# Decode attention and feed-forward on one core: two units per softmax, score products of 512 columns, V behind the next pair's K

## The chip, the core and the metric

The kernel runs on one of the eight cores of one Trainium2 chip. A core has five engines with instruction queues of their own: PE (TensorE, matrix products), DVE (VectorE), ACT (ScalarE), POOL (GpSimd) and SP (SyncE, which here issues all the transfers). Sixteen DMA engines move data between the chip's memory (HBM) and the core's on-chip memory; products are accumulated in PSUM, which has eight banks of 512 fp32 values per partition, over 128 partitions.

The metric is the device time of one execution in microseconds. Before the change three runs gave 654.61, 655.31 and 655.44 us; the median is 655.31.

## The reference: what is computed

One token of each of four sequences goes through two identical layers of attention and feed-forward (the weights and the cache of both layers are the same arrays):

```python
B, Sq, D = 4, 1, 512
Hq, Hkv, Sk, Dh = 32, 8, 8192, 128          # 4 query heads share one key/value head

def _A_ref(x, k_cache, v_cache, wq, wo):
    q = (x @ wq).reshape(B, Sq, Hq, Dh).transpose(0, 2, 1, 3)
    k = jnp.repeat(k_cache, 4, axis=1)
    v = jnp.repeat(v_cache, 4, axis=1)
    scores = jnp.einsum("bhqd,bhkd->bhqk", q, k) * (Dh ** -0.5)
    p = softmax(scores, axis=-1)
    o = jnp.einsum("bhqk,bhkd->bhqd", p, v)
    return o.transpose(0, 2, 1, 3).reshape(B, Sq, Hq * Dh) @ wo

def _B_ref(x, w_gate, w_up, w_down):        # F = 1792
    return (silu(x @ w_gate) * (x @ w_up)) @ w_down

for _ in range(2):
    x = x + _A_ref(layernorm(x), k_cache, v_cache, wq, wo)
    x = x + _B_ref(layernorm(x), w_gate, w_up, w_down)
```

All arrays are bf16. Both caches together have 4 x 8 x 8192 x 128 x 2 values, 134 MB, and each layer needs all of them.

## The kernel before, in words

**Units.** A unit is one pair of a sequence and a key/value head: 32 units per layer, numbered u = 4 * head + sequence. A unit's K is 2 MB and so is its V: 8192 rows, of which partition p holds 64 consecutive ones. On chip there are eight slots of 2 MB (`kv`, slots 0 to 7), each for one K or one V.

**Loads.** `work(L)` (L270) gives the order of a layer's K and V: K0, K1, V0, K2, V1, K3, V2 and so on; V trails K by a unit. Layer 1 begins with the units 29, 30 and 31, whose K and V stay in slots 0 to 5 from the end of layer 0 (`kept`), so only 58 of its 64 tiles are loaded. `items` is the list of all loads of both layers, with the feed-forward weights (`wg`, `wu`, `wd`) behind the last V of each. `pump()` (L316) walks along it and issues the next load on SP's queue whenever a slot is free; `finished()` (L363) frees a slot when PE has used its tile. The feed-forward weights lie in slots 6 and 7, so the last loads of a layer (`late`, L329) must take slots below 6. The last V of a layer comes in four quarters (`split`), and two tiles at the start of layer 1 come in two halves, each as soon as half of a kept K has been scored (`halves`, `half`, L350). SP executes its issues in order: a load that waits for its slot holds all the loads behind it.

**A unit's work.** `keys` (L473) cuts K into eight blocks. Per block DVE transposes 32x32 tiles in place (`turn`, L396), and PE makes four products (`scores`, L414) with the four heads' queries as the fixed operand, set by POOL into a field of zeros (`zq`, `place_q`), and 256 columns of K as the moving one. Each unit's scores fill one of two PSUM banks as 128 x 256: row 4q + h holds block q and head h. Then the softmax runs in five steps, threaded between the next unit's blocks: `max_p` (DVE, maximum per row), `max_t` (a PE transpose, a DVE maximum per head, an ACT copy), `exps` (a PE product that spreads the maximum, three ACT instructions), `turn_p` (DVE transposes P into one of two halves of `pT`), `total` (a PE sum and a DVE reciprocal). `values` (L496) multiplies P by V in 16 products that lie on four column groups of PE; ACT, DVE and one more product (`own_first`, `own_others`, `add_rows`) add up the four partial sums. The last two units of a layer use `block_last` instead, 64 small products each. After every fourth unit `out_proj` adds the head's share of the output projection to x.

**The order.** The program text decides it. Blocks wait in a list `blocks`, softmax steps in `line`, the steps behind V in `after`; each has a nominal duration, and `advance` (L382) takes steps out when enough nominal time has gone by. Transposes run ahead of the blocks by two nominal microseconds (`LAG`). `flush` forces steps out that must precede others.

**The seam.** `ffn` (L647) needs x after the last unit, so the last V, the output projection, w_gate, w_up and w_down follow each other; layer 1's first two K take slots 6 and 7, so they wait until the feed-forward's products have been made.

Of the kernel before, what the change touches and what calls it, by code (L numbers as in the profile page):

```python
# [103 lines left out]
def bass_interleave_layers__gqa_block_cached__swiglu_ffn__decode_kernel(  # L104
# [18 lines left out]
    P = 128  # L123
# [9 lines left out]
    assert NB * REP == QB and 2 * 2 * QB == Dh  # L133
    SW = TB * QB
# [7 lines left out]
    NV = NB // 2  # L142
    assert TB == 2 * NA and NV * REP <= QB
# [4 lines left out]
    with ExitStack() as es:  # L148
# [8 lines left out]
        kvf = sb("kvf", [P, NSLOT * SL + FR * F], BF16)  # L157
# [3 lines left out]
        wu_sb = [kvf[:, NSLOT * SL + k * F:NSLOT * SL + (k + 1) * F] for k in range(FR)]  # L161
        wu_sb.append(kvf[:, f0 + KT * F:f0 + (KT + 1) * F])
        f1 = f0 + (KT + 1) * F
        assert f1 + FO * D <= NSLOT * SL
# [3 lines left out]
        at_w = {"wg": room(f0, f0 + KT * F) + ["wg"], "wu": room(f0 + KT * F, f1) + ["wu", "wu3"],  # L168
# [8 lines left out]
        one = sb("one", [P, 7], FP32)  # L177
        onesf, eps_sb, lsc_sb, zero_sb, mx, nm, rs = (one[:, i:i + 1] for i in range(7))
        quad = sb("quad", [P, NA], BF16)
        head = sb("head", [P, REP], FP32)  # L180
        xs = sb("xs", [P, B], FP32)
# [6 lines left out]
        own = sb("own", [P, NV], FP32)  # L188
        xc, xx = acc[:, 0:XB], acc[:, XB:2 * XB]
        zq = sb("zq", [P, 4, ZP + P], BF16)  # L190
        m4 = sb("m4", [1, REP], FP32)
        rsm = sb("rsm", [P, REP], FP32)
        pb = sb("pb", [P, SW], BF16)
        mrow = pb[0:1, :].bitcast(FP32)
        pT = sb("pT", [P, 2, SW], BF16)
        qT = pT[:, 1, 0:XQ].rearrange("p (b h) -> p b h", b=B)
        rl = sb("rl", [P, 3, REP], FP32)
# [15 lines left out]
        def bank_bf(k):  # L213
# [14 lines left out]
                 for n, c in (("wq", KT), ("wo", 4), ("wg", 1), ("wu", 2), ("wd", 3))}  # L228
# [11 lines left out]
        for a in range(NA):  # L240
# [8 lines left out]
             reads=["ident"], writes=["head"])  # L249
        T.op("dve", lambda e: e.tensor_reduce(acc[:, 0:QB], identf[:].rearrange("p (y h) -> p y h", h=REP), AX.X, ALU.max),  # L250
             reads=["ident"], writes=["acc"])
        T.op("dve", lambda e: e.tensor_reduce(own[:], acc[:, 0:QB].rearrange("p (a y) -> p y a", a=NA)[:, 0:NV, :],
# [7 lines left out]
        turn_of = {}  # L260
        rl_of = {}
# [8 lines left out]
        def work(L):  # L270
            us, seq = unit_order[L], []
            for i, u in enumerate(us):
                seq.append(("K", L, u))
                if 1 <= i < NU - 2:
                    seq.append(("V", L, us[i - 1]))
            return seq + [("V", L, u) for u in us[NU - 3:]]
# [16 lines left out]
        def load_weight(name, i=0):  # L293
# [8 lines left out]
            elif name == "wg":  # L302
                T.dma("sp", wg_sb, B_w_gate.rearrange("(kt p) f -> p kt f", p=P), sem_w["wg"][0], writes=places + ["wg"])
            elif name == "wu":
                if i == 0:
                    T.dma("sp", kvf[:, NSLOT * SL:].rearrange("p (k f) -> p k f", k=FR),
                          B_w_up[0:FR * P, :].rearrange("(kt p) f -> p kt f", p=P), sem_w["wu"][0], writes=["wu"])
                T.dma("sp", wu_sb[FR], B_w_up[FR * P:, :], sem_w["wu"][1], writes=["wu3"])
            else:

                for j, (a, b) in enumerate(WD):
                    T.dma("sp", wd_sb[:, a:b, :].rearrange("p (m e) n -> p m (e n)", e=2),
                          B_w_down[a * P:b * P, :].rearrange("(m p e) n -> p m (e n)", p=P, e=2), sem_w["wd"][j],
                          writes=[f"wd{j}"])

        def pump():  # L316
            while issued[0] < len(items):
# [11 lines left out]
                late = any(e - 10 < n < e for e in ends)  # L329
# [52 lines left out]
        def advance(us):  # L382
            for steps in (line, after):
                if steps:
                    steps[0][0] -= us
                    while steps and steps[0][0] <= 0:
# [17 lines left out]
        def place_q(u, eng="pool", src=qr, keys_=SCR):  # L404
# [4 lines left out]
            dst = zq[:, :, ZP:].rearrange("p c (a x) -> p c a x", a=NA)[:, :, :, 0:REP]  # L409
# [4 lines left out]
        def scores(L, u, q):  # L414

            s = slot_of["K", L, u]
            bk = SBK[turn_of[u]]
            w = kv[:, s, q * TB * Dh:(q + 1) * TB * Dh].rearrange("p (t c i e) -> p t c i e", t=TB, c=2, e=2)
            z0 = ZP - REP * q
            for c in range(4):  # L420
                T.op("pe", lambda e: e.matmul(bank(bk)[:, 0:SW], lhsT=zq[:, c, z0:z0 + P], rhs=w[:, :, c // 2, :, c % 2],  # L421
                                              start=(q == 0 and c == 0), stop=(q == NB - 1 and c == 3)),
                     reads=[f"s{s}.{q}", "zq"], writes=[f"pb{bk}"], sig=(c == 3))

        def max_p(u):
            bk = SBK[turn_of[u]]
# [3 lines left out]
        def max_t(u):  # L430
# [3 lines left out]
            T.op("dve", lambda e: e.tensor_reduce(m4[:], bank(STEP)[0:1, 0:P].rearrange("p (x h) -> p h x", h=REP),  # L434
                                                  AX.X, ALU.max, negate=True),
                 reads=[f"pb{STEP}"], writes=["m4"])
            T.op("act", lambda e: e.activation(mrow.rearrange("p (x h) -> p x h", h=REP),  # L437
                                               m4[:].unsqueeze(1).to_broadcast([1, QB, REP]), ACTF.Copy),
                 reads=["m4"], writes=["pb"])

        def exps(u):
            bk = SBK[turn_of[u]]
# [3 lines left out]
            by = rstd[:, u % B:u % B + 1]  # L446
            T.op("act", lambda e: e.activation(nm[:], bank(STEP)[:, 0:1], ACTF.Copy, scale=by), reads=[f"pb{STEP}", "rstd"],  # L447
                 writes=["nm"])
            T.op("act", lambda e: e.activation(pb[:], bank(bk)[:, 0:SW], ACTF.Exp, bias=nm[:], scale=by, accum_out=rs[:]),  # L449
                 reads=[f"pb{bk}", "nm", "rstd"], writes=["pb", "rs"])  # L450
            T.op("act", lambda e: e.activation(rsm[:], head[:], ACTF.Copy, scale=rs[:]), reads=["head", "rs"], writes=["rsm"])  # L451

        def turn_p(u):
            T.op("dve", lambda e: e.transpose(pT[:, turn_of[u], :], pb[:]), reads=["pb"], writes=[f"pT{turn_of[u]}"])  # L454

        def total(u):
            T.op("pe", lambda e: e.matmul(bank(TOT)[:, 0:REP], lhsT=ones, rhs=rsm[:], start=True, stop=True),  # L457
                 reads=["rsm", "onesf"], writes=[f"pb{TOT}"])
            T.op("dve", lambda e: e.reciprocal(rl[:, rl_of[u], :], bank(TOT)[:, 0:REP]), reads=[f"pb{TOT}"],  # L459
                 writes=[f"rl{rl_of[u]}"])  # L460
# [12 lines left out]
        def keys(L, u):  # L473
            def block(q):
# [6 lines left out]
                if q == NB // 2 - 1 and ("K", L, u) in halves:  # L481
                    half(("K", L, u), 0)
                if q == NB - 1:
                    finished(("K", L, u))
                    for gap, fn in ((0.0, max_p), (1.0, max_t), (0.9, exps), (1.0, turn_p), (0.3, total)):
                        line.append([gap, u, lambda fn=fn: fn(u)])

            for q in range(NB):
                if (L, u, q) not in turned:
                    turn(L, u, q)  # L490
                blocks.append((0.65, lambda q=q: block(q)))
                drain(LAG)
# [3 lines left out]
        def values(L, u):  # L496
            g, b = unit_gb(u)
            bk = OBK[turn_of[u]]

            def begin():  # L500
                flush(line, u)
                flush(after, turn_of[u])

            def end():
                finished(("V", L, u))
                after.extend(rest)

            def block(i):
# [4 lines left out]
                v = kv[:, s, :].rearrange("p (q t d) -> p t q d", t=TB, d=Dh)  # L513
                for t in range(TB):
                    j = t % NA
                    c0 = t * QB + i * NV * REP
                    T.op("pe", lambda e: e.matmul(bank(bk)[j * QB:j * QB + NV * REP, :],  # L517
                                                  lhsT=pT[:, turn_of[u], c0:c0 + NV * REP], rhs=v[:, t, NV * i:NV * (i + 1), :],
                                                  start=(i == 0 and t == j), stop=(i == 1 and t >= TB - NA)),
# [241 lines left out]
```

## Time and profile before

| | us |
|---|---|
| median of three runs | 655.31 |
| the profiled execution, its own time | 655.51 |
| its span in the trace | 653.7 |
| PE busy, products (4896 instructions) | 500.5 |
| DVE busy (1079) | 446.1 |
| ACT busy (391) | 116.4 |
| K transposes on DVE, 488 of 686 ns | 322.4 |
| score products on PE, 2048 of 256 columns | 346.2 |
| V products, 960 of 512 columns on four column groups | 68.5 |
| P transposes on DVE, 64 of 405 ns | 25.9 |

Busy time of a pipelined PE is the time in which any product is under way; the mean duration of one product (314 ns for a score product) is longer than its share of the busy time. In the profile, "DVE kvf L401" means the DVE instruction of line 401 that writes the tile `kvf`; "<-DMA kvf<-in_A_k_cache_dram" behind a wait means that a load of K ended it. SPq is SP's queue. Granted clock is the share of full speed that the clock throttle allowed PE. HBM was read at 419 GB/s over the span, 273.88 MB in all.

### The profile page before, as it was taken

What the parts mean: (1) busy time and instruction counts of PE and PEld (TensorE: products, weight loads), DVE (VectorE), ACT (ScalarE), POOL (GpSimd) and SP (SyncE); (2) the same over time, 40 slices, a digit from 0 to 9 for tenths busy, and PEclk for the clock granted to TensorE, in tenths of its full rate; (3) what the DMA queues carried; (4) which work ended last, traced back from release to release, by engine and by line L of the source; (5) the groups of instructions that cost most, each with busy time, mean ns of one, the idle gap of its engine ahead of it and who ended that gap; (6) DMA issues with size and microseconds to landing.
All of it is one profiled execution on the core that took longest, in us unless ns stands there. A gap on an engine that the chain in (4) does not pass through costs nothing.

```text
span 653.7 us, 11807 instructions
## 1 busy us (share of the span) xinstructions
PE 500.5 (77%) x4896; PEld 319.2 (49%) x4896; DVE 446.1 (68%) x1079; ACT 116.4 (18%) x391; POOL 19.3 (3%) x73
## 2 busy tenths in 40 slices
PE   1766787977777877787876988887688787786886
PEld 1544444544444544544555655554354454443456
DVE  2556676776776777776752399996677677676682
ACT  0021121221221221221220212221122122121120
POOL 0000000000000000000000000000000000000000
PEclk9897788777978778789685989997978887797895
DMA  9999999999999999999999999999999999999996
GB/s 368 428 425 423 438 429 427 432 431 429 430 431 429 430 430 432 430 432 428 427 416 375 398 411 431 430 428 429 430 428 429 433 430 430 432 427 429 432 420 239
DMA packets 24085, 274.64 MB, mean 420 GB/s; under 512 B 2392, under 2 KB 2400, under 8 KB 7904
## 3 DMA queue, kind: packets, MB, share of 16 engines
q1 hardware_dynamic: 24032, 273.89, 98.9%
q8 instruction: 38, 0.62, 0.3%
q14 instruction: 15, 0.12, 0.0%
HBM read 273.88 MB, written 0.00 MB: 419 GB/s over the span
## 4 chain that ended last, share of the span: by engine, by line
DMA 66%; DVE 17%; PE 13%; SPq 3%; issue 1%; ACT 0%; POOL 0%; DVEq 0%; POOLq 0%
DMA kvf<-in_A_k_cache_dram 63%; DVE kvf L401 11%; PE ps L421 8%; DVE acc L531 3%; DMA kvf<-in_B_w_down_dram 3%; SPq L93 2%; PE ps L517 1%; DVE one L427 1%; DVE pT L454 1%; PE ps L587 1%; DVE m L434 1%; PE ps L625 1%; PE ps L457 0%; PE ps L676 0%; PE ps L549 0%
## 5 line engine op out<-in xcount | busy, mean ns | idle before, releaser
L401 DVE STREAM_TRANSPOSE kvf<-kvf 128x512 f32<-128x512 f32 x488 | 322.4, 686 | 121.8 <-DMA kvf<-in_A_k_cache_dram 121.8
L421 PE MATMUL ps<-kvf,zq 128*128 128x256 bf16 x2048 | 346.2, 314 | 18.2 <-DVE kvf L401 15.7
L421 PEld LDWEIGHTS ps<-kvf,zq 128*128 128x128 bf16 x2048 | 211.3, 115 | 89.8 <-DVE kvf L401 40.4
L437 ACT ACTIVATE pb<-m 1x128 f32<-1x128 f32 x64 | 19.7, 308 | 453.5 <-DVE m L434 453.5
L431 PE MATMUL ps<-identf,one 128*1 128x128 f32 x64 | 18.3, 286 | 68.3 <-DVE one L427 68.3
L517 PE MATMUL ps<-kvf,pT 128*16 128x512 bf16 x960 | 68.5, 409 | 0.9 <-DVE rl L459 0.9
L531 DVE SCALAR_TENSOR_TENSOR acc<-ps,own,acc 128x128 f32<-128x128 f32 x180 | 63.1, 351 | 6.5 <-ACT acc L526 1.9
L431 PEld LDWEIGHTS ps<-identf,one 128*1 128x1 f32 x64 | 5.1, 80 | 99.4 <-DVE one L427 93.2
L536 PE MATMUL ps<-head,acc 128*128 128x4 f32 x120 | 26.4, 290 | 17.9 <-DVE acc L531 17.7
L536 PEld LDWEIGHTS ps<-head,acc 128*128 128x128 f32 x120 | 22.8, 237 | 34.2 <-DVE acc L531 33.6
L443 PE MATMUL ps<-one,pb 1*128 1x1 f32 x128 | 27.8, 284 | 14.1 <-ACT pb L437 13.8
L443 PEld LDWEIGHTS ps<-one,pb 1*128 1x128 f32 x128 | 22.4, 217 | 32.8 <-ACT pb L437 29.1
L449 ACT ACTIVATE pb<-ps,one,rstd 128x256 bf16<-128x256 f32 x64 | 36.2, 565 | 2.1
L412 POOL TENSOR_TENSOR zq<-scr,quad 128x64 bf16<-128x64 bf16 x62 | 18.2, 293 | 608.1 <-PE ps L421 569.4
L517 PEld LDWEIGHTS ps<-kvf,pT 128*16 128x16 bf16 x960 | 19.3, 91 | 32.8 <-issue 21.2
L427 DVE TENSOR_REDUCE one<-ps 128x1 f32<-128x256 f32 x64 | 25.6, 399 | 13.1 <-PE ps L421 12.7
L454 DVE STREAM_TRANSPOSE pT<-pb 128x256 bf16<-128x256 bf16 x64 | 25.9, 405 | 1.9 <-ACT pb L449 1.9
L457 PEld LDWEIGHTS ps<-rsm,one 128*128 128x128 f32 x128 | 24.5, 237 | 3.0 <-ACT rsm L451 0.9
L457 PE MATMUL ps<-rsm,one 128*128 128x4 f32 x128 | 21.6, 239 | 0.0
L447 ACT ACTIVATE one<-ps,rstd 128x1 f32<-128x1 f32 x64 | 16.7, 261 | 25.8 <-PE ps L443 25.8
L526 ACT ACTIVATE acc<-ps,own 128x128 f32<-128x128 f32 x60 | 20.6, 343 | 0.0
L434 DVE TENSOR_REDUCE m<-ps 1x4 f32<-1x128 f32 x64 | 15.6, 244 | 6.5 <-PE ps L431 6.5
(66 smaller groups left out, 165.9 us busy)
## 6 DMA issues: line engine op xcount, KB each, us to landing
kvf<-in_A_k_cache_dram SPq DMA_DIRECT2D x60, 2048.0 KB, 30.0
kvf<-in_A_v_cache_dram SPq DMA_DIRECT2D x58, 2048.0 KB, 33.8
wq_sb<-in_A_wq_dram SPq DMA_DIRECT2D x4, 1024.0 KB, 7.6
wo_sb<-in_A_wo_dram SPq DMA_DIRECT2D x4, 1024.0 KB, 34.5
kvf<-in_A_v_cache_dram SPq DMA_DIRECT2D x8, 512.0 KB, 19.3
kvf<-in_B_w_gate_dram SPq DMA_DIRECT2D x2, 1792.0 KB, 23.2
kvf<-in_B_w_down_dram SPq DMA_DIRECT2D x4, 768.0 KB, 16.0
kvf<-in_A_v_cache_dram SPq DMA_DIRECT2D x2, 1024.0 KB, 7.0
```

The lines of the kernel that those rows point to most:

```text
L401: T.op("dve", lambda e: e.transpose(w, w), reads=[f"s{s}.{q}"], writes=[f"s{s}.{q}"])
L421: T.op("pe", lambda e: e.matmul(bank(bk)[:, 0:SW], lhsT=zq[:, c, z0:z0 + P], rhs=w[:, :, c // 2, :, c % 2], start=(q == 0 and c == 0), sto ...
L427: T.op("dve", lambda e: e.tensor_reduce(mx[:], bank(bk)[:, 0:SW], AX.X, ALU.max), reads=[f"pb{bk}"], writes=["mx"])
L431: T.op("pe", lambda e: e.matmul(bank(STEP)[0:1, 0:P], lhsT=mx[:], rhs=identf[:], is_transpose=True, start=True, stop=True), reads=["mx", " ...
L434: T.op("dve", lambda e: e.tensor_reduce(m4[:], bank(STEP)[0:1, 0:P].rearrange("p (x h) -> p h x", h=REP), AX.X, ALU.max, negate=True), rea ...
L443: T.op("pe", lambda e: e.matmul(bank(STEP)[:, 0:1], lhsT=mrow, rhs=onesf[0:1, :], start=True, stop=True), reads=["pb", "onesf"], writes=[f ...
L449: T.op("act", lambda e: e.activation(pb[:], bank(bk)[:, 0:SW], ACTF.Exp, bias=nm[:], scale=by, accum_out=rs[:]), reads=[f"pb{bk}", "nm", " ...
L454: T.op("dve", lambda e: e.transpose(pT[:, turn_of[u], :], pb[:]), reads=["pb"], writes=[f"pT{turn_of[u]}"])
L457: T.op("pe", lambda e: e.matmul(bank(TOT)[:, 0:REP], lhsT=ones, rhs=rsm[:], start=True, stop=True), reads=["rsm", "onesf"], writes=[f"pb{T ...
L517: T.op("pe", lambda e: e.matmul(bank(bk)[j * QB:j * QB + NV * REP, :], lhsT=pT[:, turn_of[u], c0:c0 + NV * REP], rhs=v[:, t, NV * i:NV * ( ...
L531: T.op("dve", lambda e: e.scalar_tensor_tensor(acc[:], bank(bk)[:, k * Dh:(k + 1) * Dh], own[:, k:k + 1], acc[:], op0=ALU.mult, op1=ALU.ad ...
L536: T.op("pe", lambda e: e.matmul(bank(LNB)[:, 0:REP], lhsT=acc[:], rhs=head[:], start=True, stop=True), reads=["acc", "head"], writes=[f"pb ...
```

## The change

Units are taken in pairs, and a pair goes through one softmax.

- The moving operand of a score product has 512 columns (16 instead of 8 of a partition's rows), so a unit has four blocks of four products instead of eight. A unit's scores fill only every other row of a 128 x 512 bank: the query field `zq` has its four heads at every other column, and the second unit of the pair is shifted by one row. Both units of a pair accumulate into the same bank; the next pair uses the other one.
- `max_p`, `max_t`, `exps`, `turn_p` and `total` run once per pair, on 512 columns and eight (head, unit) rows. The two units have different layer norm factors, so `both_deviations` puts them into alternate rows of a vector `rstd2`, once per layer.
- V is used after the next pair's K: the order of loads and of use is K0 K1 K2 K3 V0 V1 K4 K5 V2 V3 and so on, with two places of layer 1 written out differently (K31, V29, V30, K0, then K1, V31, K2, V0). P has one buffer instead of two, and `turn_p` waits in the list until both V of the pair before have been used.
- V products read every other column of P; each goes over all four partial sums of one row position t, 16 products per unit as before. `block_last` has four blocks of 16 products.
- `pb` and P together need 512 bytes more per partition. For that, the last 256 columns of the third row block of w_up have no lasting place: they lie behind w_down in slot 7 and are loaded in both layers, ahead of w_down, as a transfer of their own.
- `late` names the positions whose slots must be below 6: the three K and three V that are kept.

At the end of layer 0, V31 takes the slot of V28, as before; V28 is now used after K30 and K31 have been scored, where it was used ahead of both.

```diff
-    SW = TB * QB
+    TS = 2 * TB
+    NS = TT // TS
+    PAIR = 2 * REP
+    SW = TS * QB
...
+        def w_up(k, f):
+            if k == FR - 1 and f >= F - FC:
+                return kvf[:, f2 + f - (F - FC):f2 + FC][:, 0:2 * P - 1:2]
+            return wu_sb[k][:, f:f + 2 * P - 1:2]
...
-        pT = sb("pT", [P, 2, SW], BF16)
+        pT = sb("pT", [P, SW], BF16)
...
         def work(L):
             us, seq = unit_order[L], []
-            for i, u in enumerate(us):
-                seq.append(("K", L, u))
-                if 1 <= i < NU - 2:
-                    seq.append(("V", L, us[i - 1]))
-            return seq + [("V", L, u) for u in us[NU - 3:]]
+            for i in range(0, NU, 2):
+                ks = [("K", L, u) for u in us[i:i + 2]]
+                vs_ = [("V", L, u) for u in us[max(i - 2, 0):i]]
+                if L == 1 and i == 2:
+                    seq += [ks[0]] + vs_ + [ks[1]]
+                elif L == 1 and i == 4:
+                    seq += [ks[0], vs_[0], ks[1], vs_[1]]
+                else:
+                    seq += ks + vs_
+            return seq + [("V", L, u) for u in us[NU - 2:]]
...
+                T.dma("sp", kvf[:, f2:f2 + FC], B_w_up[(FR - 1) * P:FR * P, F - FC:], sem_w["wu"][2], writes=["wu2"])
...
-                late = any(e - 10 < n < e for e in ends)
+                late = any(n in (e - 3, e - 4, e - 5, e - 7, e - 8, e - 11) for e in ends)
...
-            z0 = ZP - REP * q
+            m, x = place[u]
+            bk = SBK[m % 2]
+            z0 = ZP - (PAIR * q + x)
             for c in range(4):
                 T.op("pe", lambda e: e.matmul(bank(bk)[:, 0:SW], lhsT=zq[:, c, z0:z0 + P], rhs=w[:, :, c // 2, :, c % 2],
-                                              start=(q == 0 and c == 0), stop=(q == NB - 1 and c == 3)),
+                                              start=(x == 0 and q == 0 and c == 0), stop=(x == 1 and q == NS - 1 and c == 3)),
...
-                    for gap, fn in ((0.0, max_p), (1.0, max_t), (0.9, exps), (1.0, turn_p), (0.3, total)):
-                        line.append([gap, u, lambda fn=fn: fn(u)])
+                    if x == 1:
+                        for gap, fn in ((0.0, max_p), (1.3, max_t), (0.9, exps), (1.25, turn_p), (0.3, total)):
+                            ready = (lambda: before_used(m)) if fn is turn_p else (lambda: True)
+                            line.append([gap, m, lambda fn=fn: fn(m), ready, m])
...
-                for t in range(TB):
-                    j = t % NA
-                    c0 = t * QB + i * NV * REP
+                n = TS // 2
+                for t in range(i * n, (i + 1) * n):
+                    j = t % NA
+                    w = pT[:, t * QB + x:(t + 1) * QB:2]
...
+        def both_deviations(L):
+            for k in range(2):
+                b0, b1 = (u % B for u in unit_order[L][2 * k:2 * k + 2])
+                T.op("dve", lambda e: e.tensor_scalar(rstd2[:, k:k + 1], rstd[:, b0:b0 + 1], side[:, 0:1], None, op0=ALU.mult),
+                     reads=["rstd", "side"], writes=["rstd2"])
+                T.op("dve", lambda e: e.scalar_tensor_tensor(rstd2[:, k:k + 1], rstd[:, b1:b1 + 1], side[:, 1:2],
+                                                             rstd2[:, k:k + 1], op0=ALU.mult, op1=ALU.add),
+                     reads=["rstd", "side", "rstd2"], writes=["rstd2"])
```

## The prediction, made before the changed kernel ran

> **What bounds the kernel now.** I read the page's shares first, then its slices and DMA queues, then the chain, then windows and the timeline at the seams.
>
> ```profile
> span 653.7 us, 11807 instructions
> ...
> PE 500.5 (77%) x4896; PEld 319.2 (49%) x4896; DVE 446.1 (68%) x1079; ACT 116.4 (18%) x391; POOL 19.3 (3%) x73
> ...
> GB/s 368 428 425 423 438 429 427 432 431 429 430 431 429 430 430 432 430 432 428 427 416 375 398 411 431 430 428 429 430 428 429 433 430 430 432 427 429 432 420 239
> ...
> q1 hardware_dynamic: 24032, 273.89, 98.9%
> q8 instruction: 38, 0.62, 0.3%
> ...
> DMA 66%; DVE 17%; PE 13%; SPq 3%; issue 1%; ACT 0%; POOL 0%; DVEq 0%; POOLq 0%
> ```
>
> The data queue fills 98.9% of the DMA engines' time, and the slices stand at 430 GB/s except at the start, at the layer seam (slices 21 to 24) and at the end. The landing events of the trace give the rate directly: each 2 MB load lands 4.86 us after the one before it, in both layers. PE at 77% and DVE at 68% lie beside that, so a faster score or softmax shortens nothing while loads are queued. Time can be won or lost only where a load starts late, where one DMA engine is later than the rest, and behind the last load. Windows:
>
> ```profile
> 345.00:350.00 5.00, 2.38 (x80) 2.29 (x80) 1.56 (x6) 0.25 (x1) 0.00 (x0) 0.50 0.81 310
> 350.00:355.00 5.00, 2.61 (x68) 2.21 (x66) 1.59 (x10) 0.00 (x0) 0.00 (x0) 0.50 1.01 375
> 355.00:360.00 5.00, 4.83 (x31) 3.74 (x32) 0.24 (x2) 0.56 (x2) 0.00 (x0) 0.66 1.02 428
> 360.00:365.00 5.00, 4.50 (x39) 3.36 (x37) 1.15 (x3) 1.52 (x5) 0.29 (x1) 1.00 0.91 316
> ...
> 385.00:390.00 5.00, 4.34 (x39) 3.10 (x35) 4.92 (x13) 1.77 (x6) 0.00 (x0) 1.00 0.97 377
> ...
> 645.00:654.00 9.00, 5.79 (x174) 5.37 (x174) 2.91 (x13) 0.81 (x3) 0.00 (x0) 0.50 0.24 87
> ```
>
> The last two columns are the DMA share and GB/s: the engines run dry shortly at 345 to 350, 360 to 365 and 385 to 390, the restart of layer 1, and behind 645, where only the feed-forward remains. The timeline names the links there:
>
> ```profile
> 338.75 0.59 PE L549 MATMUL ps<-pT,kvf 128*128 128x4 bf16 x16 [0.56 <-DMA kvf<-in_A_v_cache_dram]
> ...
> 347.31 1.63 PE L659 MATMUL ps<-xn,kvf 128*128 128x4 bf16 x56 [2.34 <-DMA kvf<-in_B_w_up_dram]
> ...
> 349.02 3.44 SPq L93 DMA_DIRECT2D kvf<-in_A_k_cache_dram  x2
> ```
>
> The last V quarter of layer 0 ends the attention, w_up holds the feed-forward, and only then SP issues layer 1's first K. So the seam is a chain of loads with the slowest DMA engine setting it. How slow that is, the landing events tell: the sixteen engines land the first K within 0.60 us of each other, but the last V quarter of layer 0 between 333.76 and 338.70, and the last of layer 1 between 634.96 and 639.93. The spread grows in steps of 1.2 to 1.5 us, one engine at a time, a few us after each packet of q8 (28.4, 36.9, 58.4 us and so on); some eight engines take turns.
>
> **The change, part by part.** The sum is made against this execution: span 653.7, execution 655.51, so 1.8 lie around it; the median of the runs, 655.31, is 0.2 below.
>
> *Scores, softmax, V order (hidden, 0).* 2048 score products of 256 columns become 1024 of 512. Streaming at full clock, 8 of them took 1.05 us and 12 took 1.50, so 112 ns each; 512 columns are bounded by 224 ns (twice that) and 338 ns (twice 346.2/2048). Per unit 3.6 to 5.4 us against 5.4 now. Per pair DVE loses one max, one small max and one reciprocal, but the 512-wide ones grow: max 0.40 to between 0.40 and 0.80, P's transpose 0.41 to between 0.41 and 0.81; I take 0.66 for both (each 256 columns add 0.27 at 1 ns a column, the rest is fixed). Per pair that is 16 x 0.62 + 0.66 + 0.24 + 0.66 + 0.15 + 2 x (1.12 + 0.13) = 14.1 us under 19.4 us of loading. The cover is 20 us of queued loads (median 30 us from issue to landing); if it is gone, each us costs a us.
>
> *Order of slots (hidden in mid-stream).* A K is freed some 10 (first) or 17 us (second of the pair) after the pair's first K lands, its V at 18 and 19; the load that reuses the slot is due to start 34 us after. No starvation from this.
>
> *Setup and both_deviations (0).* Two reductions and four DVE instructions of about 0.2 us, while the queue is full.
>
> *Fewer PE instructions.* PE had 4896 products and as many weight loads. Scores drop 1024, the three softmax steps 32 + 64 + 64: 3712 remain, 7424 instructions for 9792. At 38 packets for 9792 (258 each) that makes 29. From 350 us to the last V, 17 q8 packets fell on some eight engines, so one took three (4.97 is 0.6 and three steps); with 13 none need take more than two. One step of 1.3 us goes from the slowest engine: -1.35 (ends 0, if the steps have another cause or are hidden, and -2.7).
>
> The Trainium skill (Runtime: NRT & Kernel Launch, Instruction fetch mechanics) says that an engine's instructions come in 16 KiB blocks of 256 and that crossing a block is mostly hidden. The block size agrees with 0.62 MB in 38 packets; by "hidden" this term would be 0 and the sum -0.4. The landing steps speak against it, as the fetch costs the DMA engine and not PE.
>
> *w_up's tail.* Columns 1536 on of its third row block are loaded in each layer: 64 KB more in layer 1, 8 rows of 512 bytes per engine. By packets of 2 KB (84 ns) and 1 KB (46 ns) a row takes between 21 and 46 ns: +0.2 (0.2 to 0.4), directly ahead of w_down.
>
> *The seam of layer 0.* V31 waits for V28's slot, as before, but V28 is now used behind K30 and K31. Before, V28 was multiplied from 318.96 and V31 issued at 320.09, long before V30 had landed (332.54). Now, from K30's landing (about 312.8, the same place in the stream) DVE has 16 transposes 9.9, max 0.66, small max 0.24 with a round trip to PE 0.45, weighted adds 2.2, P 0.66, the output projection's two steps 0.9, the rest 0.3: 15.3; then the last score block 1.05 and V28's products 1.0, with up to 1.7 of handshakes: issue at 330.1 to 331.8. From issue to first byte 2.0 to 2.7 us (349.02 to a landing at 355.88 less 4.86; 384.17 to 391.72 less 4.86). All engines start V31 at 332.1 to 334.5; the slowest started at 332.54 before. SP holds V31, then w_gate, w_up, w_down, all behind this wait, and PE waits for each; so the delay passes on whole. Against it, the fast engines' lead was worthless anyway, and the step that fell into V31 at 336.7 (1.2 us) need not. I take +0.5 (ends -1.2 and +2.5).
>
> *Restart of layer 1.* Before, the first engine's landings of ten loads after K0 (355.88 to 406.32) took 50.4 against 48.6: 1.8 idle, on the slowest engine 51.2. Now K2 and V0 come in halves into K29's and K30's slots as these are scored, in one run; the next load takes K31's slot, after the pair's max has been threaded through K31: 364.8 + 0.5 (query placed) + 16 x 0.225 + 0.9 of softmax steps = 369.8, first byte 372.3, where the stream is free at 371.1. Idle about 1.2. K0's slot (383) and K1's (389.4, by 16 transposes and the softmax behind each other) are due at 384 and 389.5: just in time. -0.6 (ends -1.8; +2 if both are late).
>
> *Behind the last V.* Before, the last quarter of V28, here the last V, landed at 639.93 and its scaling began at 641.94, 2.0 later with 40 products left, where layer 0 took 0.68. With whole quarters as blocks that becomes 0.7, but then w_down holds the end: its last piece landed at 649.86, the last sum began at 650.88; in layer 0 the sum was done 0.7 after. -0.5 (0 to -0.6).
>
> Sum: -1.35 + 0.2 + 0.5 - 0.6 - 0.5 = -1.75. Span 652.0, execution 653.8, median **653.6 us**. About 0.2% (1.3 us) is what a measurement can tell here.
>
> **The rivals.**
> 1. *As summed*: 653.6, own range 652.3 to 654.9. For it: the steps follow the packets. Chance 0.50.
> 2. *Fetches cost nothing, the rest cancels*: without the first term -0.4, 654.9. For it: several steps are smaller (0.4) and come without a q8 packet. It is also what the Trainium skill's page named above would give. Chance 0.18.
> 3. *Slower: V31 waits.* V28's products in layer 0 are the place. From an issue at 331.0 on, the middle of what I take, every us passes through the seam. PE's granted clock was 0.53 from 310 to 320; at that clock the 16 V products took 1.88 us where they take 1.04, the last score block would take 0.9 more, and handshakes double (+1.3): issue near 334.0, 656.6. It decides the sign from an issue at about 332.7 on. Against it: the clock was 0.91 and 1.00 from 320 to 330. Chance 0.20.
> 4. *More than summed*: layer 1 restarts without idling and the engines keep together within 2.3 us: a further -1.8, 651.8. Against it: K31's slot comes late by the working above. Chance 0.12.
>
> That the change doesn't do what it says is part of 2: two halves at 112 ns or one at 224 is the same stream.
>
> **How the numbers follow.** Of 1, six tenths lie under 654.0: 0.31, with 4 and a tenth of 2 faster 0.45; slower are nine tenths of 3 and a little of 2, 0.21; the rest, 0.34, is within. The range reaches to rivals 4 and 3: 651.6 to 656.8.
>
> **What would show it.** Right: q8 near 29 packets; landing spread of the last V under 4 us; last V under 639.5; V31 issued 330 to 332; w_down, not PE, ahead of the last sum. Wrong: slices under 425 GB/s in mid-stream, V31 issued behind 332.7, K0's and K1's successors late with windows at 370 to 395 under 400 GB/s, or the spread as before with fewer packets.

## The result and the profile after

The changed kernel is slower: 662.89 us (four runs, 662.57 to 663.40) against 655.38 us, a ratio of 1.0116 (95% interval 1.0099 to 1.0134). The prediction was 653.6 with a range to 656.8; the time is outside it, and on the other side of the kernel before. The profiled execution took 662.91 us; its span is 661.1 us against 653.7.

The page of the changed kernel: shares, rate in 40 slices, queues, chain.

```profile
span 661.1 us, 9243 instructions
...
PE 464.8 (70%) x3712; PEld 197.5 (30%) x3712; DVE 431.0 (65%) x961; ACT 78.8 (12%) x231; POOL 19.8 (3%) x73
...
GB/s 367 428 428 423 436 427 431 433 427 434 427 428 434 428 433 430 428 432 429 406 339 383 366 427 430 429 430 433 428 429 431 431 431 428 431 431 429 433 415 145
...
q1 hardware_dynamic: 24336, 273.96, 98.0%
q8 instruction: 29, 0.48, 0.3%
...
DMA 56%; PE 23%; DVE 18%; SPq 1%; issue 1%; ACT 1%; POOL 0%; DVEq 0%; POOLq 0%
```

Mid-stream is as fast as before: a load still lands 4.86 us after the one before it, so pairing and 512 columns cost nothing there, and PE's busy time fell from 500.5 to 464.8 us. The loss is in slices 20 to 23 (the seam: 406, 339, 383, 366 where 427, 416, 375, 398 stood) and in the last one (145 for 239). In the chain 10 points have moved from DMA to PE.

The landings in the two traces place it, in us. Each of the sixteen DMA engines brings a part of every load; an engine's lag is the time by which its part lands after the first engine's, and the spread of a load is the lag of its slowest engine.

| | before | after | difference |
|---|---|---|---|
| V31 of layer 0 issued | 320.09 | 331.53 | |
| w_up landed, last engine | 347.18 | 350.01 | +2.8 |
| layer 1's first K issued | 349.02 | 351.97 | +3.0 |
| last V landed, first engine | 634.96 | 638.50 | +3.5 |
| last V landed, last engine | 639.93 | 643.59 | +3.7 |
| end of the span | 653.7 | 661.1 | +7.4 |

So 3.0 us are lost at the seam, 0.7 from there to the last V (0.4 of it in the first ten loads of layer 1), and 3.7 behind the last V, where the end now comes 17.5 us after the landing instead of 13.8. (The kernel before was profiled once more below; there it was 14.7.) Windows of the changed kernel at the seam (PE, PEld, DVE, ACT and POOL busy, PE's clock, DMA share, GB/s):

```profile
325.00:330.00 5.00, 3.90 (x46) 1.68 (x45) 3.40 (x8) 0.00 (x0) 0.00 (x0) 1.00 0.89 380
330.00:335.00 5.00, 3.24 (x40) 1.25 (x37) 2.54 (x6) 2.11 (x6) 0.00 (x0) 1.00 0.54 155
335.00:340.00 5.00, 3.27 (x86) 3.12 (x86) 1.86 (x8) 0.37 (x1) 0.00 (x0) 0.54 1.02 395
```

The kernel before moved 432, 404 and 414 GB/s in the same windows, the second of them being

```profile
330.00:335.00 5.00, 5.00 (x85) 3.66 (x86) 2.99 (x9) 2.01 (x7) 0.00 (x0) 1.00 0.98 404
```

What the DMA engines wait for is V31's load, and the timeline of the changed kernel shows why it is late:

```profile
328.24 2.23 PE L444 MATMUL ps<-kvf,zq 128*128 128x512 bf16 x8 [0.59 <-DVE kvf L423]
330.39 1.47 PE L557 MATMUL ps<-kvf,pT 128*16 128x512 bf16 x24
...
331.53 1.75 SPq L93 DMA_DIRECT2D kvf<-in_A_v_cache_dram  x4
```

K31's last score blocks (L444) come first, then V28's products (L557; the row also holds the first eight of V29's), and only then can SP issue V31 into V28's slot. V30, the load before, had landed on the first engine at 328.81.

The end, again the changed kernel's timeline:

```profile
635.12 2.23 PE L444 MATMUL ps<-kvf,zq 128*128 128x512 bf16 x8 [0.21 <-DVE kvf L423]
...
637.39 0.69 DVE L450 TENSOR_REDUCE one<-ps 128x1 f32<-128x512 f32 x1 [1.13 <-PE ps L444]
...
640.37 0.78 ACT L472 ACTIVATE pb<-ps,one 128x512 bf16<-128x512 f32 x1
...
641.27 0.71 DVE L483 STREAM_TRANSPOSE pT<-pb 128x512 bf16<-128x512 bf16 x1 [0.97 <-ACT pb L472]
...
642.13 1.39 PE L587 MATMUL ps<-pT,kvf 128*128 128x4 bf16 x48
...
644.39 1.12 DVE L569 SCALAR_TENSOR_TENSOR acc<-ps,own,acc 128x128 f32<-128x128 f32 x3 [0.23 <-ACT acc L564]
...
647.63 0.59 PE L627 MATMUL ps<-o,wo_sb 128*128 128x4 bf16 x16 [0.28 <-DVE o L624]
648.08 1.42 PE L587 MATMUL ps<-pT,kvf 128*128 128x4 bf16 x48
...
649.54 0.17 DVE L594 TENSOR_TENSOR oT<-ps,rl 128x4 bf16<-128x4 f32 x1 [1.11 <-PE ps L587]
```

K28, the last K, landed at 624.0 but was scored only at 637.3. Then come the pair's one softmax with nothing beside it (637.39 to 642.0), V27's products, V26's weighted sums (L569), head 6's output projection (L627), and only then three quarters of the last V's products, whose data had been there since 643.59. The kernel before scaled the last unit 2.0 us after the landing; here it is 6.0 (L594 at 649.54).

### The profile page after: what moved, and what is told of

It reads as the page before. It is cut to its first block, busy times and chain, and to the rows that moved or that the text cites. A ratio compares the mean times of both kernels' runs of the same rounds, so it can differ in the third digit from the quotient of the medians.

```text
span 661.1 us, 9243 instructions
## 1 busy us (share of the span) xinstructions
PE 464.8 (70%) x3712; PEld 197.5 (30%) x3712; DVE 431.0 (65%) x961; ACT 78.8 (12%) x231; POOL 19.8 (3%) x73
## 4 chain that ended last, share of the span: by engine, by line
DMA 56%; PE 23%; DVE 18%; SPq 1%; issue 1%; ACT 1%; POOL 0%; DVEq 0%; POOLq 0%
DMA kvf<-in_A_k_cache_dram 53%; PE ps L444 13%; DVE kvf L423 11%; PE ps L557 3%; DMA kvf<-in_B_w_down_dram 2%; DVE acc L569 2%; DVE one L450 1%; SPq L93 1%; PE ps L574 1%; PE ps L674 1%; DVE pT L483 1%; PE ps L466 1%; PE ps L627 1%; PE ps L454 1%; PE ps L587 1%
## 5 line engine op out<-in xcount | busy, mean ns | idle before, releaser
L423 DVE STREAM_TRANSPOSE kvf<-kvf 128x512 f32<-128x512 f32 x488 | 307.6, 677 | 101.4 <-DMA kvf<-in_A_k_cache_dram 101.4
L444 PE MATMUL ps<-kvf,zq 128*128 128x512 bf16 x1024 | 317.7, 444 | 66.8 <-DVE kvf L423 36.2
L444 PEld LDWEIGHTS ps<-kvf,zq 128*128 128x128 bf16 x1024 | 95.9, 112 | 235.5 <-DVE kvf L423 93.3
L557 PE MATMUL ps<-kvf,pT 128*16 128x512 bf16 x960 | 67.5, 404 | 2.5 <-DMA kvf<-in_A_v_cache_dram 2.5
L569 DVE SCALAR_TENSOR_TENSOR acc<-ps,own,acc 128x128 f32<-128x128 f32 x180 | 60.2, 334 | 5.1 <-ACT acc L564 0.5
L574 PE MATMUL ps<-head,acc 128*128 128x4 f32 x120 | 24.9, 278 | 13.0 <-DVE acc L569 12.2
L594 DVE TENSOR_TENSOR oT<-ps,rl 128x4 bf16<-128x4 f32 x64 | 9.7, 152 | 31.8 <-PE ps L574 28.7
L557 PEld LDWEIGHTS ps<-kvf,pT 128*16 128x16 bf16 x960 | 18.5, 88 | 34.0 <-issue 14.9
L450 DVE TENSOR_REDUCE one<-ps 128x1 f32<-128x512 f32 x32 | 21.1, 661 | 10.8 <-PE ps L444 10.8
L460 ACT ACTIVATE pb<-m 1x128 f32<-1x128 f32 x32 | 9.9, 308 | 139.2 <-DVE m L457 139.2
L472 ACT ACTIVATE pb<-ps,one 128x512 bf16<-128x512 f32 x32 | 24.9, 778 | 1.1
L483 DVE STREAM_TRANSPOSE pT<-pb 128x512 bf16<-128x512 bf16 x32 | 21.6, 676 | 4.2 <-ACT pb L472 4.0
L457 DVE TENSOR_REDUCE m<-ps 1x8 f32<-1x128 f32 x32 | 8.9, 277 | 14.6 <-PE ps L454 14.6
L466 PEld LDWEIGHTS ps<-one,pb 1*128 1x128 f32 x64 | 11.8, 229 | 20.2 <-issue 18.0
L466 PE MATMUL ps<-one,pb 1*128 1x1 f32 x64 | 14.5, 293 | 0.3 <-ACT pb L460 0.3
```

The costliest lines, as they stand in the source:

```text
L423: T.op("dve", lambda e: e.transpose(w, w), reads=[f"s{s}.{q}"], writes=[f"s{s}.{q}"])
L450: T.op("dve", lambda e: e.tensor_reduce(mx[:], bank(bk)[:, 0:SW], AX.X, ALU.max), reads=[f"pb{bk}"], writes=["mx"])
L466: T.op("pe", lambda e: e.matmul(bank(STEP)[:, 0:1], lhsT=mrow, rhs=onesf[0:1, :], start=True, stop=True), reads=["pb", "onesf"], writes=[f ...
L483: T.op("dve", lambda e: e.transpose(pT[:], pb[:]), reads=["pb"], writes=["pT"])
L557: T.op("pe", lambda e: e.matmul(bank(bk)[j * QB:j * QB + NS * REP, :], lhsT=w, rhs=v[:, t, :, :], start=(t == j), stop=(t >= TS - NA)), re ...
L569: T.op("dve", lambda e: e.scalar_tensor_tensor(acc[:], bank(bk)[:, k * Dh:(k + 1) * Dh], own[:, k:k + 1], acc[:], op0=ALU.mult, op1=ALU.ad ...
```

## The experiments

**1. The two ends, one at a time.** Theory A: the seam's loss is V31's wait behind K31, the end's is the uncovered softmax. The first edit moves V28 ahead of K31 in layer 0 alone:

```diff
+                elif L == 0 and i == NU - 2:
+                    seq += [ks[0], vs_[0], ks[1], vs_[1]]
...
```

(In layer 0 the position that `late` names for K31 moves along, as K31 is kept and must take a slot below 6.)

> At the end of layer 0, V28 is loaded and used ahead of K31 instead of behind it; nothing else moves. Theory A (the seam's 3 us are the wait of V31's load for V28's products, which stand behind K31): V31 is issued at 321 to 325 instead of 331.5, the windows 325 to 335 carry over 420 GB/s instead of 380 and 155, layer 1's first K is issued near 349.5 instead of 351.97, and the time falls by 2 to 3 us, to 660 to 661. Rival B (the fast engines' lead is worth nothing, only the slowest engine's start counts, 332.5 instead of 333.75): at most 1.2 us, 661.7. Rival C (the last pair's softmax, behind K31 that now comes 4.86 us later, ends the attention): V31's products end behind 341.4 and the time is as now, 662.9, or longer.

Measured: 658.14 us, ratio 1.0040 (1.0028 to 1.0053), 4.7 us less than the changed kernel's 662.89. V31 is issued right behind V28's products, five microseconds earlier, and the DMA engines do not run dry:

```profile
325.00:330.00 5.00, 4.63 (x39) 2.18 (x36) 3.71 (x9) 0.37 (x1) 0.00 (x0) 0.66 0.99 406
330.00:335.00 5.00, 3.60 (x28) 1.26 (x28) 2.34 (x5) 0.75 (x3) 0.00 (x0) 1.00 0.99 405
```

```profile
325.87 0.61 PE L560 MATMUL ps<-kvf,pT 128*16 128x512 bf16 x8
...
326.57 1.76 SPq L93 DMA_DIRECT2D kvf<-in_A_v_cache_dram  x4
```

Layer 1's first K is issued at 348.10, 3.9 us earlier and even 0.9 earlier than before the change. Theory A holds for the seam; rival B (1.2 us at most) and rival C fall. Not all of A's figures came: V31 was issued later than its 321 to 325 and the windows stayed under 420 GB/s, yet layer 1's first K came earlier than its 349.5 and the gain is more than its 2 to 3 us. The end is still 18.5 us behind the last V.

The second edit changes the end of layer 1 alone, so that the last K has five V behind it:

```diff
+                elif L in (1,) and i == NU - 2:
+                    v2 = seq[-2:]
+                    seq[-2:] = [ks[0], v2[0], ks[1], v2[1]] + vs_
```

> At the end of layer 1 alone, the order K27 V23 K28 V24 V25 to V28 instead of V23 V24 K27 K28 V25 to V28: the last K lands one load (4.86 us) earlier, so five V instead of four lie behind it. Theory A (behind the last V the end waits for the last pair's softmax, which starts when K28 is scored at 637.3): the transposed P of the last pair is ready by 637 instead of 642, the span ends 13.8 to 14.8 us behind the last V's landing instead of 17.5, and the time falls by 2.7 to 3.7 us, to 659.2 to 660.2. Rival D (PE's clock of 0.5 and the output projection ahead of the last products are what is slow): P is earlier, but the end comes at least 16 us behind the last landing, under 1.5 us gained.

Measured: 662.19 us, ratio 1.0105 (1.0081 to 1.0128): no gain that can be told. The end is 16.4 us behind the last V, as rival D expected. (PE's clock, which D names, is not the difference between the kernels: it was 0.50 from 645 to 654 us in both.) The softmax does come earlier, but not by what it could: its PE step (L457) stands behind V26's products, which wait for their load, and V27's products wait for the weighted sums (L572) of the V before:

```profile
633.58 1.89 PE L560 MATMUL ps<-kvf,pT 128*16 128x512 bf16 x16 [2.29 <-DMA kvf<-in_A_v_cache_dram]
635.39 0.37 PE L457 MATMUL ps<-identf,one 128*1 128x128 f32 x1
...
640.57 1.42 PE L590 MATMUL ps<-pT,kvf 128*128 128x4 bf16 x48 [1.34 <-DVE acc L572]
```

The third edit is that order in both layers (with `late` moved along in layer 0):

> The last pair's two K come earlier in both layers (layer 0: K30 V26 K31 V27 V28 to V31), so V28 is used right behind V27, and the last softmax has five V behind its K. Theory A: both ends are repaired, the sum of the two runs above, 5 to 6.5 us: 656.4 to 657.9; what is left against the kernel before is w_up's tail (0.2) and the restart of layer 1 (0.5). Rivals B, C and D: less than 3 us in all, over 660.

Measured: 655.67 us, ratio 1.0006 (0.9996 to 1.0016): the whole loss is gone, 0.7 us better than A's lower end, though the end is still 16.3 us behind the last V. Since the layer 1 edit gained nothing beside the late seam, something else at the end had to be found.

**2. What stands behind the last V.** Theory E: the weighted sums of V25 and V26 and the output projection of head 6. The edit gives the last four V instead of two the small products, which need no sums (in both layers, with the orders of the third run; then in layer 1 alone, as `[-(2, 4)[L]:]`; then in both, with the first run's order in layer 0 and the second's in layer 1):

```diff
-            if u in unit_order[L][-NLAST:]:
+            if u in unit_order[L][-4:]:
```

> As the order with the last pair's K earlier in both layers, and the last four V of a layer (instead of two) use the small products of block_last, so no weighted sums of V25 and V26 (ACT, three on DVE, a product, a scaling, each waiting for the one before) stand ahead of V28's blocks. Theory E (those sums and the output projection of head 6, queued ahead of V28's last blocks, are the 2.5 us that the end still had over the kernel before): the span ends 13.8 to 14.5 us behind the last V instead of 16.3, the time is 652.8 to 653.8, below the kernel before. Rival (192 more small products per layer cost PE as much as the sums did, or the feed-forward is what is long): 655 or more, the end 16 us or more behind the last V.

Measured: 654.52 us, ratio 0.9987 (0.9976 to 0.9997). The end is 13.5 us behind the last V, and PE now waits for loads at each step, V27, V28's last quarter and w_down:

```profile
635.40 2.29 PE L591 MATMUL ps<-pT,kvf 128*128 128x4 bf16 x80 [1.17 <-DMA kvf<-in_A_v_cache_dram]
...
640.35 0.59 PE L591 MATMUL ps<-pT,kvf 128*128 128x4 bf16 x16 [0.60 <-DMA kvf<-in_A_v_cache_dram]
...
649.86 1.01 PE L730 MATMUL ps<-scr,kvf 128*128 128x4 bf16 x32 [0.33 <-DMA kvf<-in_B_w_down_dram]
```

The time is 0.7 us above the upper end of what was expected. In the profiled execution (655.72 us, the slowest of ten) the slowest engine landed the last V 5.67 us behind the first; whether that holds for the median is not shown. PE has 184 products more than in the third run over both layers, not 192 in each.

> The changed kernel, with the small products for the last four V of layer 1 alone; orders as they are. Theory E: P of the last pair still comes at 642, but behind it only V27, the output projection of head 6 and V28 remain: scaling at 647.1 instead of 649.5 where the stream is as it was, the end 15 to 15.5 us behind the last V instead of 17.5, time 660.4 to 661. Rival (the softmax behind the last K alone is what is exposed): within 0.5 us of 662.9.

Measured: 662.61 us, ratio 1.0121 (1.0104 to 1.0138): no gain, as the rival expected. In the profiled execution (661.45 us, the fastest of four) the chain became shorter as worked out (V28's scaling at 646.48, 10.2 us behind the start of the last pair's maximum at 636.27, where it was 12.2 behind, 637.39 to 649.54), but PE then stood 1.3 us in the output projection with nothing named that it waited for:

```profile
647.40 0.54 PE L627 MATMUL ps<-o,wo_sb 128*128 128x4 bf16 x14 [0.29 <-DVE o L624]
649.28 0.19 PE L627 MATMUL ps<-o,wo_sb 128*128 128x4 bf16 x2 [1.34 <-issue]
```

and the seam was the latest of all runs that have it (V31 issued at 332.92). A packet of q8, the queue of instruction fetches, had ended at 647.92, 1.36 us before PE went on, so a late fetch would fit; it is not shown, as most such packets go by without a wait of PE.

> Layer 0 ends with V28 ahead of K31, layer 1 with the last pair's K earlier, the last four V of both layers by small products. Theory: the seam as with V28 ahead of K31 alone (layer 1's first K issued at 348 to 349 instead of 351.97), the end 13.8 to 14.5 us behind the last V: 652 to 653.5. Rival (K31, now one load later, and the small products hold the end of layer 0's attention behind the weights): layer 1's first K issued behind 349.5 and the time over 654.

Measured: 654.66 us, ratio 0.9990 (0.9977 to 1.0002). The end is 14.1 us behind the last V, but layer 1's first K is issued at 350.37. The rival was right on both of its signs, a first K behind 349.5 and a time over 654. The run of part 3, which differs from this one only in having the small products for two V of layer 0 instead of four, issued it at 348.07, so those products are at least part of the delay.

> The changed kernel once more, unchanged, to see what repeats of it on this chip: time 662.6 to 663.4. If the seam's loss is the wait of V31 it repeats (V31 issued between 331 and 333, layer 1's first K at 351.5 to 353.5); the spread of the last V's landing, if it is set by which engine the fetches happen to fall on, differs from 5.1 (the three kernels before this with the same 29 packets had 3.3 to 4.2).

Measured: 660.84 us, ratio 1.0094 (1.0079 to 1.0109), 1.8 us less than the least that was expected. V31 was issued at 332.01 and layer 1's first K at 351.63: the seam's loss repeats. The lag of the slowest engine at the last V was 4.55. The end was 15.8 us behind the last V instead of 17.5; V28's scaling began 2.4 us earlier, at 647.18. Where these 2.4 us come from the timelines tell, of the first execution,

```profile
619.17 1.31 DVE L423 STREAM_TRANSPOSE kvf<-kvf 128x512 f32<-128x512 f32 x2 [5.16 <-DMA kvf<-in_A_k_cache_dram]
...
625.15 1.87 PE L444 MATMUL ps<-kvf,zq 128*128 128x512 bf16 x4
```

and of the second:

```profile
617.54 1.31 DVE L423 STREAM_TRANSPOSE kvf<-kvf 128x512 f32<-128x512 f32 x2 [5.09 <-DMA kvf<-in_A_k_cache_dram]
...
623.11 1.03 PE L444 MATMUL ps<-kvf,zq 128*128 128x512 bf16 x4
```

DVE waits for K27's landing, and from there on the end is one chain of work: 16 transposes, softmax, sums, projection, feed-forward. K27's slowest engine was 1.6 us earlier, and one more block of scores ran in 1.03 us instead of 1.87. The difference goes with PE's granted clock: it was 0.50 over the slow block and 1.00 over the fast one. Of the last pair's eight blocks, four were slow in the first execution, three in the second and six in the run with V28 first; the span ended 42.0, 41.3 and 42.9 us behind K27's landing. (In the kernel before it was 33.4, with one load less behind K27, 4.86 us.) So the changed kernel's own end varies by as much as the two single edits (16.4 and 15.9 us) could show. Whether both together do better, with the seam left as it is, was then run:

> The changed kernel with both edits at the end of layer 1 (the last pair's K earlier, small products for the last four V) and the end of layer 0 as it is. If the two things behind the last V stand in series, so that each edit alone only uncovered the other (16.3 and 15.9 us behind the last V, no gain in time that could be told from the changed kernel's own 15.8 to 17.5), both together give 13.5 to 14.2 us and a ratio to the kernel before of 1.004 to 1.007, where the changed kernel had 1.0094 and 1.0116: what then remains is the seam. If not: the ratio stays at 1.008 or more.

Measured: 659.36 us, ratio 1.0062 (1.0048 to 1.0076), 13.5 us behind the last V, with V31 issued at 332.47 and layer 1's first K at 352.51. PE waits for loads again, the last quarter of V28 and w_gate:

```profile
644.34 0.59 PE L590 MATMUL ps<-pT,kvf 128*128 128x4 bf16 x16 [0.61 <-DMA kvf<-in_A_v_cache_dram]
...
648.71 0.91 PE L712 MATMUL ps<-xn,kvf 128*128 128x4 bf16 x28 [1.11 <-DMA kvf<-in_B_w_gate_dram]
```

The two obstacles stand in series: with the K alone earlier, the sums and the projection hold V28; with the sums alone away, the softmax does. The distance of the end from w_down's last landing, the last load of all, says it more plainly than that from the last V: 3.9 and 3.4 us in the two executions of the kernel before, 7.4 and 5.4 in those of the changed kernel, 6.1 with the K alone earlier, 5.5 with the sums alone away, 3.4 with both. By ratios the parts add up: from the changed kernel's 1.0105 (mean of its two) the end of layer 1 takes 0.0043 (2.8 us), the seam 0.0065 (4.3 us), which leaves 0.9997.

**3. A version of the best parts.** Layer 0 as in the first run, layer 1 as in the run just told.

> Layer 0 ends as in the run with V28 ahead of K31 (small products for its last two V only), layer 1 with the last pair's K earlier and small products for its last four V. If the two ends add up: layer 1's first K is issued near 348.1, the end comes 13.5 to 14.2 us behind the last V, 652.5 to 653.8, faster than the kernel before by 0.2 to 0.4%. If the start of layer 1 and the lag of the slowest engine move as much by themselves as the ends differ now: no better than 654.5.

Measured: 654.85 us, ratio 1.0001 (0.9990 to 1.0012). Layer 1's first K was issued at 348.07 and the end came 13.9 us behind the last V, both as expected, and yet the time is that of the kernel before: the second expectation was right. With both ends mended, here and in the runs above, the ratios lie between 0.9987 and 1.0006: the change is then worth about nothing.

**4. Are fetched instructions worth time?** The term that carried the forecast was that PE's instructions are fetched in packets (q8) and that each packet sets a DMA engine back.

> 2112 small products that add zero (28 x 4, some 30 ns each) are put between the score products of pairs 2 to 12 of both layers, so PE has 4224 instructions more and q8 should fetch 45 or 46 packets instead of 29. If each fetch sets one DMA engine back by 1.2 to 1.5 us and eight engines take turns, layer 1 has some 20 instead of 12 before the last V, the slowest engine takes one more: spread of the last V's landing 6.3 us or more instead of 5.1, the last V later by about 1.3 us, time 664.2. If the steps have another cause or are made good: spread 4.5 to 5.6, time within 0.6 us of 662.9.

Measured: 717.14 us, ratio 1.098. This run answers nothing on the lag: the small products (28 columns wide) added 77 ns each to PE's busy time ((626.5 - 464.8) us over 2112), PE became the bound (88% busy), and the engines ran dry and fell into step (the last V's spread was 0.56 us). It bears out the count, 46 packets. A smaller dose, with a cheaper product (14 ns each by PE's busy time, (485.4 - 470.6) us over 1056):

```diff
+                for k in range(2 if 2 <= m < NU // 2 - 3 and c < 3 else 0):
+                    T.op("pe", lambda e: e.matmul(bank(bk)[:, 0:4], lhsT=ident, rhs=zq[:, 0, 0:4],
+                                                  start=False, stop=False),
+                         reads=["zq", "ident"], writes=[f"pb{bk}"], sig=False)
```

> The kernel of the run before this one, with 1056 small products that add zero among the score products of pairs 2 to 12 of both layers: 2112 PE instructions more, q8 at 38 or 39 packets as before the change, instead of 30. If each packet sets back one engine by 1.2 to 1.5 us: the sum of the sixteen engines' lags at V30 of layer 0 is about 33 us, as in the kernel before, where the kernels with 29 to 31 packets had 22 to 29. If the slowest engine followed the packets, as the prediction's term had it, the last V would come 1.3 us later and the time would be 1 to 1.5 us longer; if not, within 0.6 us of the run before this one.

Measured: 656.36 us against 654.85, on one chip; ratios 1.0018 (1.0009 to 1.0027) and 1.0001 (0.9990 to 1.0012), so 1.1 to 1.5 us more for eight packets more, what was expected if the slowest engine followed the packets. Page of this kernel, then of the one without the products:

```profile
PE 485.4 (74%) x4860; PEld 236.9 (36%) x4860; DVE 428.6 (65%) x955; ACT 78.2 (12%) x229; POOL 19.8 (3%) x73
...
q8 instruction: 38, 0.62, 0.3%
```

```profile
PE 470.6 (72%) x3804; PEld 202.1 (31%) x3804; DVE 428.9 (66%) x955; ACT 78.2 (12%) x229; POOL 19.8 (3%) x73
...
q8 instruction: 30, 0.49, 0.3%
```

The sixteen engines' lags at V30 of layer 0 add up to 30.3 us instead of 23.7 (33 was expected). The slowest engine at the last V lags 5.15 us instead of 4.42. Where the two traces part (2.1 us in all) speaks against PE's time in mid-stream: V30 landed first at 328.97 against 329.10, and in layer 1 the time from the eleventh load to the last V was 228.8 against 228.7. They part by 1.1 us at the seam, where the slowest engine's lag grew by 0.9 us during w_up, by 0.6 from there to the eleventh load of layer 1, and by 0.7 in the last V's spread, less 0.5 behind it. That is one execution of each.

> The kernel before, unchanged, for a second look at its lags: sum at V30 of layer 0 near 33.8 us and slowest engine at the last V near 5.0 if they are set by the program; a different slowest engine's lag, by up to 1.5 us, if they are set by where the packets happen to fall.

Measured: 655.85 us. The sum at V30 was 32.1 us (33.8 in the first execution), the slowest engine at the last V 3.31 (4.97): in these two executions the sum stays with the program, while the slowest engine differs.

## Why the prediction was wrong, point by point

The terms summed to -1.75 us and the span grew by 7.4. Of the 9.1 us between, 4.2 are the end (wrong in sign), 2.5 the seam (right in sign, too small), 1.35 the fetch term (not seen) and 1.0 the restart of layer 1 (wrong in sign).

**Scores, softmax, V order (hidden, 0).** Right in mid-stream (4.86 us per load; the sizes were near, maximum 0.66 and P's transpose 0.68 us, both taken as 0.66). Wrong as a single term: "if it is gone, each us costs a us" was not applied to the two places where no queued loads lie beside it, the ends of the layers. That is where the loss came from.

**The seam of layer 0 (+0.5; measured +3.0).** The mechanism and the place were right, and even the issue (330.1 to 331.8; it was 331.53, and 332.0 to 332.9 in four further runs with the same layer 0). The step that failed is "the fast engines' lead was worthless anyway", and with it the price, "decides the sign from an issue at about 332.7 on", and the credit for the step that "need not" fall into V31. In five executions with this seam, layer 1's first K followed V31's issue by 19.6 to 20.6 us; to reach the 349.02 of the kernel before, V31 would, by this estimate, have had to be issued near 328.8 and to start, counted by landings, near 331.0 (2.2 us later: the first quarter landed at 334.99 and takes 1.25). That is not when the slowest engine ends V30 (332.5) but close to when the mean engine does (330.6: 328.81 and a sixteenth of the summed lags of 28.2 us). No run issued V31 between 326.6 and 331.5, so the limit itself was not measured. The windows say the same: their DMA shares from 325 to 340 are 0.89, 0.54 and 1.02 against 1.01, 0.98 and 1.02, so the mean engine lost (0.12 + 0.44) x 5 = 2.8 us, and w_up landed 2.8 us later. Over the five executions, windows to 345, the loss is 2.9 to 4.5 us and w_up's delay 2.5 to 4.2; in the first experiment the shares are 0.99, 0.99 and 1.02. The credit did not come: the engines, all idle before, started V31 together (spread 0.81 us), and the next setback made one of them the slowest. Behind a q8 packet at 342.8 the spread grew from 0.73 at V31's last quarter to 2.28 at w_gate, and in four of the five executions it grew by 1.0 to 1.6 there; in the first experiment, with engines 3.2 us apart, a packet at 342.3 left w_up's spread at 3.2.

**Behind the last V (-0.5; measured +3.7, and +2.0 in the second execution).** Wrong in sign, also against the 14.7 us of the kernel before's second execution. "That becomes 0.7" took the last V's landing for the last event. The softmax of the last pair, V26's sums and the projection of head 6 were behind it. The term looked at how blocks of V are cut, not at where the last pair's softmax now lies; the runs with the K earlier, with the sums away and with both show that both obstacles must go.

**Fewer PE instructions (-1.35).** The packets came out as counted (29), and in the pair of runs made for it eight packets more went with 1.1 to 1.5 us more. The failing step is "one step goes from the slowest engine": in the changed kernel's execution the last V's spread was 5.09 us with 29 packets, and in nine further executions with 29 to 31 it was 3.2 to 5.7. That the kernel gains by it on average is likely from that pair, not shown: the extra products also add PE time, 14.8 us of it, and at the restart and the seam part of the 1.1 to 1.5 is not excluded as PE's. The Trainium skill (Runtime: NRT & Kernel Launch, Instruction fetch mechanics) has a block crossing mostly hidden. If the 1.1 to 1.5 us are the packets', it was not hidden in this pair of runs.

**Restart of layer 1 (-0.6; measured +0.4,** 50.88 us for ten loads against 50.44). K31's slot was taken at 372.94; the 369.8 of the working and the seam's 3.0 make 372.8, so that step held. What failed is "in one run": the halves of K2 and V0 landed 3.08, 2.88, 2.85 and 2.45 us after one another, where 2.43 is the stream, 1.5 us idle in all. The load into K31's slot added 0.7 (5.56 us after the one before it, not 4.86), where 1.2 was worked out.

**w_up's tail (+0.2)** landed 0.20 us behind the piece before it in layer 0 and 0.19 in layer 1. **Order of slots** and **setup** held.

Of the rivals, the third had the right sign and the right place at the seam, and too small a price; none had the end.

## What to carry to other kernels

A reordering that is free while loads are queued is not free at the two ends of the stream, so walk the last loads by name: when is each operand's last user done, what softmax or sum follows it, and what stands between the last landing and its use. When a stream's DMA engines are out of step, do not take the slowest engine's end as the time by which the next load must be there: here, by estimate, the mean engine's end was nearer, and the idle time of all engines together gave the loss. And of two obstacles in series, removing one can show no gain: try both before ruling either out.

## What had not been expected of the hardware

- The lag of the slowest DMA engine differs by up to 1.7 us between two executions of one program (4.97 and 3.31), while the sum over all engines stays within 2 us at V30 (33.8 and 32.1; 28.2 and 26.7 in the changed kernel).
- The granted clock falls differently in two executions of one program: four score products of 512 columns took 1.03 us at 1.00 and 1.87 at 0.50 in the same place; four or three of the eight blocks of the last pair were slow. Where PE's work is exposed, such a block is 0.84 us.
- Small products into a bank that is being accumulated added 77 ns each to PE's busy time with a fixed operand of 28 columns, four at a time, and 14 ns with one of 128 columns, two at a time. Which of the differences matters was not tried.
